# A fused attention and feed-forward kernel: turns of eight steps instead of four, V read per quad, two banks for set-aside scores, and the change of rows behind a GpSimd instruction

## The chip, the core and the metric

The kernel runs on one core of one Trainium2 chip. The metric is the device time of one execution in microseconds (us); lower is better. The engines are named as in the profile: PE (TensorE matmuls), PEld (its weight loads), DVE (VectorE), ACT (ScalarE), POOL (GpSimd) and SP (SyncE, which here only issues DMAs).

## What is computed

The layer norm of x feeds an attention of 32 heads of 16 dimensions over 2048 tokens, and a feed-forward part with squared ReLU that gates it:

```python
x = A_x                                    # [1, 2048, 512]
xn = _layernorm(x, axis=-1)
qkv = (xn @ wqkv) -> q, k, v               # H = 32 heads, Dh = 16
p = softmax(q @ k.T * Dh ** -0.5)
s = (p @ v) @ wo
r = relu(xn @ w1 + b1)                     # F = 1792
g = silu((r * r) @ w2 + b2)
out = x + s * g
```

Everything is fp32. Products of the linear parts and the scores are made with numbers split into a high and a low fp32r part (three products for one, hi-hi, hi-lo, lo-hi); the product of the exponentials with V is a plain fp32 matmul.

## The kernel before

**Setup** (to about 148 us) normalizes and transposes x, makes V, K and Q of all heads, keeps V in SBUF (tile `vt`, 16 key blocks of 560 columns: 17 per head, the 17th being one, which gives the softmax sums) and writes K and Q to memory.

**The loop.** Heads go by quads (four heads, 64 rows of K in split form for two of them, so that two heads' scores run side by side on the two halves of the PE array). A *step* is one quad, one block of 512 queries and one block of 128 keys: 8 x 4 x 16 = 512 steps. Each step has two *pairs* p = 0, 1, and each pair two halves `hp` (rows 0-63 and 64-127 of the array). `scores(i, p)` makes a direct pair into a two-bank PSUM tile S, of which there are two; `exps` then takes the exponential of the 1024 columns on ACT into a tile P in SBUF. `aside(i, p, hp)` makes one half of a pair into the single bank `lin`, and DVE copies it to P, where ACT later works in place. `values(i)` multiplies a step's four tiles with V; its 32-column tiles run four side by side and add up in the bank `acc` over the 16 key blocks.

The loop is written out by hand in *turns* of four steps (128 of them). A turn makes six direct pairs and two set-aside pairs; between them, `lin` issues products of the feed-forward part or of the output projection (*blocks*) on whichever half is given; the last two direct pairs are exponentiated while PE does the four steps' values. ACT's set-aside exponentials also run then. So PE alternates between a score part, on two 64-row halves, and a value part, on four 32-column tiles.

A pair of blocks fills two banks (`spare`). Half products of rows 0-63 of one block go to its bank while rows 64-127 of the other go to the other bank. `swap()` exchanges the rows. Before, `swap` falls on the end of a turn (a pair takes two turns), with the values between the two phases; a pair that must fit into one turn (`m == 1`, four times) gets two whole-array products (`issue_whole`) around the exchange. In other turns one product is cut into two pieces of 256 columns (`issue_part`). At the end of a pair `evict` runs on DVE: bias and ReLU, square, and the split of the hidden layer (low part on GpSimd), or the sum into `y`.

`fill` lists what a turn works on, `per` is its length for one block of 512 tokens, and `events` holds DMAs and small work by turn number (`at(time, ...)`, half numbers for after the products): loads of K (`load_ka`) and Q (`load_qa`), `split_piece` (weights cast on DVE, low part on GpSimd, next piece loaded), the row sums of the softmax (`finish`, `load_sums`, `rowsums`), the check of V's maximum (`maxvalue`), the gate (`gate_start` on ACT, `gate_end` on DVE). `see` makes ACT and DVE read one element of a tile, so that they have passed certain waits before the next instructions; which turns have it is chosen case by case.

`finish(i)` copies `acc` to `ou` once per block of queries, every fourth turn, on DVE or, in the turns with `turn_ends_first`, on ACT.

Of the kernel before, what the change touches and what calls it, by code (L numbers as in the profile page):

```python
# [36 lines left out]
NQ = H // 4  # L37
NC = S // 512
NK = S // 128
VW = 560  # L40
Z_MIN, BIG = 1e-18, 1e18
# [6 lines left out]
def mha_ffn_kernel(ctx: ExitStack, tc: tile.TileContext, x, wqkv, wo, bx, w1, b1, w2, b2, out):  # L48
# [8 lines left out]
    vt = keep.tile([128, NK, VW], FT, name="vt")  # L57
# [4 lines left out]
    qdram = [[dram.tile([128, 2, 512], FT, name=f"qd{g}_{c}") for c in range(NC)] for g in range(4)]  # L62
    xdram = [dram.tile([128, 2, 4, 512], FT, name=f"xd{c}") for c in range(3)]
# [7 lines left out]
    general_path(tc, dram, nvalid, ident, vt, kdram, qdram, gdram, x, wo, out)  # L71


def fast_path(tc, sb, ps, env):
    nc = tc.nc
    ident, vt, nvalid, stat = (env[n] for n in ("ident", "vt", "nvalid", "stat"))
    kdram, qdram, xdram, udram, zdram, gdram = (
        env[n] for n in ("kdram", "qdram", "xdram", "udram", "zdram", "gdram"))
# [4 lines left out]
    BUFS = dict(S=3, KA=3, QA=2, P=8, T=2, ou=2, wr=2, u=2, st=2, mv=2, rs=2, zc=2, rc=2)  # L83
# [68 lines left out]
    def split_w(which, ks=range(4), parts="hl"):  # L152
        if which not in wsp:
            tiles = [[t([128, 2, 512], FR, f"{w_tags[which]}{p}{i}") for i in range(2)] for p in "hl"]
            wsp[which] = [[a[k // 2][:, k % 2] for k in range(4)] for a in tiles]
# [90 lines left out]
    def end_value(c, i, v):  # L246
        pv = v[0]
        run(v[1])
        cast(act if i % 2 else dve,
             vt[:, 4 * c + i, :H * 17].rearrange("p (h e) -> p h e", e=17)[:, :, :DH],  # L250
             pv.rearrange("p (h e) -> p h e", e=DH))

    def keyquery(c, g, which, tag="S"):
# [4 lines left out]
        ev = t([128, 2, 512], FR, ("P2", "P3", "P4", "P0", "P5", "P1", "T", "T")[n] if c == 3 else f"P{n % 4}")  # L258
# [19 lines left out]

    steps = [(qd, qc, kb) for qd in range(NQ) for qc in range(NC) for kb in range(NK)]
# [12 lines left out]
    def place(i, p):  # L292
        ptile[i, p] = t([128, 2, 512], FT, f"P{2 * ((i - 1) % 4) + p}")
# [10 lines left out]
    def aside(i, p, hp):  # L304

        if hp == 0:
            place(i, p)
        score(i, p, hp, single)
        dve.tensor_copy(ptile[i, p][:, hp], single)  # L309
# [5 lines left out]
    class Block:  # L315
# [10 lines left out]
        def issue(self, half, bank):  # L326

            n, other = self.at[half], 1 - half
            if n == len(self.todo[half]):
# [4 lines left out]
            mm(bank, self.lhs(a, k)[r], self.rhs(b, k)[r], start=n == 0 and self.at[other] == 0,  # L334
               stop=n == len(self.todo[half]) - 1 and self.at[other] > 0)
            return True

        def issue_whole(self, bank):

            n = len(self.todo[0]) - 1  # L340
            k, a, b = self.todo[0].pop()
            assert (k, a, b) == self.todo[1].pop() and n in self.at and 0 in self.at
            mm(bank, self.lhs(a, k), self.rhs(b, k), start=False, stop=False)  # L343

        def issue_part(self, half, bank, part):

            n = self.at[half]
            if n >= len(self.todo[half]):
                return
            assert 0 < n < len(self.todo[half]) - 1  # L350
            k, a, b = self.todo[half][n]
            r, c = slice(64 * half, 64 * half + 64), slice(256 * part, 256 * part + 256)
            self.at[half] += part
            mm(bank[:, c], self.lhs(a, k)[r], self.rhs(b, k)[r, c], start=False, stop=False)  # L354
# [4 lines left out]
    pair, swapped = [None], [0]  # L359

    def lin(*halves):
        if pair[0]:
            for half in halves:
                j = half ^ swapped[0]
                pair[0][j].issue(half, lin_banks[j])

    def lin_part(half, part):
        if pair[0]:
            j = half ^ swapped[0]
            pair[0][j].issue_part(half, lin_banks[j], part)  # L370
# [30 lines left out]
    def split_piece(eng=None):  # L401
# [5 lines left out]
        wf[layer, m] = [t([128, 4, 256] if layer == 1 else [128, 2, 512], FR, f"wf{layer}{p}{q}") for p in "hl"]  # L407
# [40 lines left out]
    for c in ORDER:  # L448
        for m, (g, _) in enumerate(PAIRS):
            fill += [(lambda m=m: first(m), False), (None, True)]  # L450
            if m in (1, 2, 4, 6):
                for i in range(2):
                    make = lambda c=c, g=g if m > 1 else 0, i=i: second(c, g, i)
                    fill += [(make, True)] if m == 1 else [(make, False), (None, True)]
    per = len(fill) // NC
    fill = [(*a, n % per in (0, 2, 4, 5, 6, 8, 10, 12, 14, 16, 18, 20, 22, 24)) for n, a in enumerate(fill)]
# [6 lines left out]
    for i in range(4):  # L463
        part = vt[:, 4 * i:4 * i + 4]
        pool.memset(part[:, :, :H * 17].rearrange("p k (h e) -> p k h e", e=17)[:, :, :, DH:], 1.0)
        pool.memset(part[:, :, H * 17:], 0.0)
# [50 lines left out]
    for c in range(NC):  # L517
# [15 lines left out]
        for g in range(4):  # L533
# [15 lines left out]
            if g == 3 and c == 2:  # L549
                turn["KA"] = 1  # L550
                load_ka(0, 0)
                load_qa(0, 0)
            if g == 1 and c == 3:
# [11 lines left out]
    acc = [None]  # L565
# [484 lines left out]
```

## Time and profile before

| what | value |
|---|---|
| time, median of 3 runs | 1251.16 us (1250.55 to 1251.58) |
| profiled execution, its own time | 1251.08 us |
| its span | 1249.3 us |
| granted PE clock, mean | 0.997 |
| DMA moved | 137.28 MB, 84936 packets |

The span is what lies between the first and the last instruction that the profiler saw. In the groups by line, the columns are the line, the engine, the operation, what is written and read with its form, the count, then the busy time and the mean duration of one in nanoseconds, then the idle time of the engine before these instructions and what ended it. In the timeline the columns are start and duration in microseconds, engine, line, operation and tiles; `x3` joins three of them in a row. A plain fp32 matmul leaves two records, so that 16 value products are 32 of them.

### The profile page before, as it was taken

How to read it: one execution, taken by the hardware profiler on the slowest of the kernel's cores; microseconds unless marked ns; L12 is line 12 of the kernel's file. 1: busy time of each engine (PE TensorE's matmuls, PEld its weight loads, DVE VectorE, ACT ScalarE, POOL GpSimd, SP SyncE). 2: the span in 40 equal slices, each digit the busy share in tenths (PEclk: the TensorE clock that was granted, in tenths of full speed). 3: DMA queues.
4: the chain of work that ended last, by engine and by line, in shares of the span. 5: the costliest groups of instructions: out<-in, count | busy, mean ns of one | idle time of the engine just before them, and what ended most of it. 6: DMA issues, size and time to landing. Idle time of an engine off the chain costs nothing.

```text
span 1249.3 us, 24460 instructions
## 1 busy us (share of the span) xinstructions
PE 1238.0 (99%) x10029; PEld 718.9 (58%) x10029; DVE 692.9 (55%) x1274; ACT 1056.5 (85%) x1230; POOL 258.8 (21%) x151
## 2 busy tenths in 40 slices
PE   9999999999999999999999999999999999999997
PEld 8888755555555455555555555555555555555554
DVE  5543255555555655555565555555655545566655
ACT  4222599999999999999999999999999999999994
POOL 5000122122211221302023221220330212322112
PEclk9999999999999999999999999999999999999998
DMA  7555613231233232121423121332222122463445
GB/s 280 207 228 199 215 47 106 60 94 47 91 128 111 60 96 65 50 88 50 157 77 111 45 93 61 94 128 84 69 75 85 53 90 61 145 220 118 152 133 120
DMA packets 84936, 137.28 MB, mean 110 GB/s; under 512 B 26058, under 2 KB 40408, under 8 KB 83284
## 3 DMA queue, kind: packets, MB, share of 16 engines
q1 hardware_dynamic: 81668, 126.25, 31.5%
q0 software_dynamic: 2720, 8.65, 2.4%
q8 instruction: 79, 1.29, 0.4%
q10 hardware_dynamic: 432, 0.79, 0.2%
q14 instruction: 37, 0.30, 0.1%
HBM read 94.24 MB, written 41.41 MB: 109 GB/s over the span
## 4 chain that ended last, share of the span: by engine, by line
PE 98%; DVE 1%; ACT 0%; issue 0%; POOL 0%; DVEq 0%; POOLq 0%; ACTq 0%
PE acc L573 37%; PE spare L334 25%; PE S L286 16%; PE S L111 10%; PE lin L286 7%; PE spare L354 1%; PE lin L472 1%; PE S L208 0%; PE acc L111 0%; PE spare L343 0%; DVE P L309 0%; PE lin L111 0%; ACT P L290 0%; PE S L699 0%; PE acc L699 0%
## 5 line engine op out<-in xcount | busy, mean ns | idle before, releaser
L290 ACT ACTIVATE P<-S 128x1024 f32<-128x1024 f32 x768 | 733.1, 1020 | 39.5 <-PE S L286 38.4
L309 DVE COPY P<-lin 128x512 f32<-128x512 f32 x512 | 353.9, 691 | 312.9 <-PE lin L286 277.9
L573 PE MATMUL acc<-P,vt 128*32 128x512 f32 x4096 | 466.0, 595 | 0.0
L286 PE MATMUL S<-QA,KA 64*128 64x512 f32 x1536 | 335.5, 413 | 0.0
L290 ACT ACTIVATE P<-P 128x1024 f32<-128x1024 f32 x256 | 271.0, 1058 | 26.0 <-DVE P L309 19.3
L573 PEld LDWEIGHTS acc<-P,vt 128*32 128x32 f32 x4096 | 120.9, 109 | 264.8 <-issue 263.7
L286 PEld LDWEIGHTS S<-QA,KA 64*128 64x128 f32 x1536 | 153.8, 183 | 168.3 <-ACT P L290 128.1
L286 PE MATMUL lin<-QA,KA 64*128 64x512 f32 x512 | 204.0, 398 | 0.7 <-DVE P L309 0.4
L104 POOL TENSOR_TENSOR wf1l<-wr,wf1h 128x1024 fp32r<-128x1024 f32 x28 | 66.8, 2384 | 400.9 <-DVE wf1h L100 136.6
L104 POOL TENSOR_TENSOR hl<-T,hh 128x1024 fp32r<-128x1024 f32 x28 | 67.3, 2405 | 236.8 <-PE S L286 152.1
L104 POOL TENSOR_TENSOR wf2l<-wr,wf2h 128x1024 fp32r<-128x1024 f32 x28 | 66.6, 2380 | 201.2 <-PE acc L573 136.4
L334 PE MATMUL spare<-xl,wf1h 64*128 64x512 f32 x440 | 105.3, 391 | 0.0
L286 PEld LDWEIGHTS lin<-QA,KA 64*128 64x128 f32 x512 | 94.2, 184 | 17.6 <-DVE P L309 2.8
L334 PE MATMUL spare<-xh,wf1h 64*128 64x512 f32 x504 | 95.8, 390 | 0.0
L334 PE MATMUL spare<-xh,wf1l 64*128 64x512 f32 x504 | 95.6, 391 | 0.0
L334 PE MATMUL spare<-wf2l,hh 64*128 64x512 f32 x400 | 93.9, 391 | 0.0
L799 DVE TENSOR_TENSOR seen<-P,S 1x1 f32<-1x1 f32 x107 | 15.1, 141 | 137.6 <-ACT P L290 137.6
L334 PE MATMUL spare<-wf2h,hh 64*128 64x512 f32 x448 | 85.9, 390 | 0.0
L334 PE MATMUL spare<-wf2h,hl 64*128 64x512 f32 x416 | 80.9, 391 | 0.0
L334 PEld LDWEIGHTS spare<-xh,wf1h 64*128 64x128 f32 x504 | 59.9, 185 | 10.1
L98 ACT CAST P<-S 128x512 fp32r<-128x512 f32 x30 | 17.6, 587 | 56.7 <-PE S L111 54.9
L334 PEld LDWEIGHTS spare<-xh,wf1l 64*128 64x128 f32 x504 | 59.9, 185 | 7.5
(220 smaller groups left out, 1197.1 us busy)
## 6 DMA issues: line engine op xcount, KB each, us to landing
wr<-in_B_w_dram SPq DMA_DIRECT2D x56, 512.0 KB
KA<-kd SPq DMA_DIRECT2D x64, 256.0 KB
QA<-qd SPq DMA_DIRECT2D x128, 128.0 KB
kd<-P SPq DMA_DIRECT2D x15, 512.0 KB
qd<-P SPq DMA_DIRECT2D x15, 512.0 KB
u<-ud SPq DMA_DIRECT2D x15, 512.0 KB
P<-in_A_x_dram SPq DMA_DIRECT2D x8, 512.0 KB
xd<-KA SPq DMA_DIRECT2D x4, 1024.0 KB
```

Source lines behind the costliest of these rows:

```text
L98: act.copy(dst, src)
L104: leng.tensor_tensor(lo, src, hi.bitcast(FT), op=OP.subtract)
L111: mm(dst, lhs(a, k), rhs(b, k), start=n == 0, stop=n == len(todo) - 1)
L286: mm(dst, k[r, p, 128 * (kb % 8):128 * (kb % 8) + 128], q[r, p], start=True, stop=True)
L290: act.activation(ptile[i, p], src, AF.Exp, scale=SCALE)
L309: dve.tensor_copy(ptile[i, p][:, hp], single)
L334: mm(bank, self.lhs(a, k)[r], self.rhs(b, k)[r], start=n == 0 and self.at[other] == 0, stop=n == len(self.todo[half]) - 1 and self.at[othe ...
L354: mm(bank[:, c], self.lhs(a, k)[r], self.rhs(b, k)[r, c], start=False, stop=False)
L472: mm(idle[:, :128], ident, ident, start=True, stop=True)
L573: mm(acc[0][32 * j:32 * j + 32], vt[:, kb, o:o + 32], ptile[i, j // 2][:, j % 2], start=kb == 0, stop=kb == NK - 1)
L799: dve.tensor_tensor(seen[:, 8:9], last, other[:1, 0, :1], op=OP.max)
```

## The change

A turn has eight steps (64 turns). Its order is spelled in two strings: S a direct pair, L two half products, 0 and 1 a set-aside half beside a half product, B both set-aside halves of a pair, / the swap, E the end of a first pair of blocks. Eleven of the 16 pairs are direct and five set aside, the halves 0 in the bank `acc` and the halves 1 in `lin` (`sides`). The values of all eight steps follow and add up in `sides[0]`; ACT copies it to `ou` after each turn, and GpSimd adds the two of a block of queries. The swap comes in mid-turn, behind a one-element `memset` on GpSimd that waits for both blocks' products so far and for which the first products on the changed rows wait. There are 16 tiles of exponentials; to make room, V is written to memory in setup and loaded per quad, two buffers of 83 columns for each key block; the first layer's split weights have one buffer instead of two (with `split_piece` ahead of the eviction in turns that need it), and the normalized attention outputs have other tiles. `see` is the same in every turn. Events move to the new turn numbers.

```diff
+QW = 83
-    vt = keep.tile([128, NK, VW], FT, name="vt")
+    vdram = dram.tile([NK, 128, VW], FT, name="vd")
     def end_value(c, i, v):
         pv = v[0]
         run(v[1])
-        cast(act if i % 2 else dve,
-             vt[:, 4 * c + i, :H * 17].rearrange("p (h e) -> p h e", e=17)[:, :, :DH],
+        n = 4 * c + i
+        vb = vblocks[n % 6]
+        cast(act if i % 2 else dve, vb[:, :H * 17].rearrange("p (h e) -> p h e", e=17)[:, :, :DH],
              pv.rearrange("p (h e) -> p h e", e=DH))
+        sp.dma_start(vdram[n], vb)
...
+    def load_v(qd):
+        vq[qd] = t([128, NK, QW], FT, "V")
+        sp.dma_start(vq[qd], vdram[:, :, 68 * qd:68 * qd + QW].rearrange("k p e -> p k e"))
...
-        ptile[i, p] = t([128, 2, 512], FT, f"P{2 * ((i - 1) % 4) + p}")
+        ptile[i, p] = t([128, 2, 512], FT, f"P{2 * ((i - 1) % 8) + p}")
...
-        score(i, p, hp, single)
-        dve.tensor_copy(ptile[i, p][:, hp], single)
+        score(i, p, hp, sides[hp])
+        dve.tensor_copy(ptile[i, p][:, hp], sides[hp])
...
-            mm(bank, self.lhs(a, k)[r], self.rhs(b, k)[r], start=n == 0 and self.at[other] == 0,
-               stop=n == len(self.todo[half]) - 1 and self.at[other] > 0)
+            ins = mm(bank, self.lhs(a, k)[r], self.rhs(b, k)[r], start=n == 0 and self.at[other] == 0,
+                     stop=n == len(self.todo[half]) - 1 and self.at[other] > 0)
+            if n == 0 and self.at[other]:
+                tc.add_manual_dep(ins.ins, fence[0], SYNC, reason="the other rows of the bank")
+            self.last = ins.ins.name
...
     def swap():
         if pair[0]:
-            while any([pair[0][half ^ swapped[0]].issue(half, lin_banks[half ^ swapped[0]]) for half in range(2)]):
+            while lin(0, 1):
                 pass
-            swapped[0] ^= 1
-            if not swapped[0]:
-                pair[0][0].evict()
-                pair[0] = None
+            f = pool.memset(note, 0.0)
+            for block in pair[0]:
+                tc.add_manual_dep(f.ins, block.last, SYNC, reason="the products so far")
+            swapped[0], fence[0] = 1, f.ins.name
+
+    def end_pair():
+        if pair[0]:
+            while lin(0, 1):
+                pass
+            swapped[0], last, pair[0] = 0, pair[0], None
+            last[0].evict()
...
     def values(i):
         qd, qc, kb = steps[i]
-        if kb == 0:
-            acc[0] = t([128, 512], FT, "acc")
         for j in (1, 2, 3, 0) if i % 2 else (0, 1, 2, 3):
-            o = (4 * qd + j) * 17
-            mm(acc[0][32 * j:32 * j + 32], vt[:, kb, o:o + 32], ptile[i, j // 2][:, j % 2],
-               start=kb == 0, stop=kb == NK - 1)
+            mm(sides[0][32 * j:32 * j + 32], vq[qd][:, kb, 17 * j:17 * j + 32], ptile[i, j // 2][:, j % 2],
+               start=kb % 8 == 0, stop=kb % 8 == 7)
...
         ou = t([128, 512], FT, "ou")
-        cast(act if turn_ends_first[0] else dve, ou, acc[0])
+        act.copy(ou, sides[0])
+        if n % 2 == 0:
+            part[0] = ou
+            return
+        pool.tensor_tensor(ou, ou, part[0], op=OP.add)
...
-    def see(i, other, act_waits, dve_waits):
+    def see(i):
         last = ptile[i, 1][:1, 1, 511:]
-        if act_waits:
-            act.copy(seen[:, :1], last)
-        if dve_waits:
-            dve.tensor_tensor(seen[:, 8:9], last, other[:1, 0, :1], op=OP.max)
+        act.copy(seen[:, :1], last)
+        dve.tensor_tensor(seen[:, 8:9], last, sides[1][:1, :1], op=OP.max)
...
+    ORDINARY = "SLLSBLLLSLL0SL1LSLL/SBLLSLL0SL1LSLL0L1SLS"
+    TWO_PAIRS = "LSLLBLLLSS/L0LL1SLLESBSLLSLLLL/SBSLLL0LL1SS"
     for n in range(TURNS):
-        i = 4 * n
+        i = 8 * n
         happen(n)
...
+        if n:
+            see(i - 1)
+        pairs = [(k, p) for k in range(i + 1, i + 9) for p in range(2)]
+        direct, asides = pairs[:9] + pairs[14:], pairs[9:14]
+        later, aside_at = [], [0, 0]
+        for row in TWO_PAIRS if makes else ORDINARY:
+            if row == "S":
+                k, p = direct.pop(0)
+                sc = scores(k, p)
+                if k == i + 8:
+                    later.append((k, p, sc))
+                else:
+                    exps(k, p, sc)
+            elif row == "L":
+                lin(0, 1)
+            elif row in "01B":
+                for hp in (0, 1) if row == "B" else (int(row),):
+                    aside(*asides[aside_at[hp]], hp)
+                    aside_at[hp] += 1
+                if row != "B":
+                    lin(1 - int(row))
+            elif row == "/":
+                swap()
+                if n == TURNS - 1:
+                    make_on(2, 3)
+            else:
+                end_pair()
+                pair[0] = makes.pop(0)()
+        for j, (k, p) in enumerate(asides):
+            exps(k, p, ptile[k, p])
+            if j == 0:
+                for fn, a in middle.pop(n, ()):
+                    fn(*a)
+        for a in later:
+            exps(*a)
...
+        pieces_now = pieces_of[n] if n < len(pieces_of) else 0
+        ahead = pieces_now > 0 and n % per in (0, 1, 3, 6, 7, 10, 11)
+        while lin(0, 1):
+            pass
+        if ahead:
+            split_piece()
+        end_pair()
...
         happen(n + 0.5)
-        if split_now:
+        for _ in range(pieces_now - ahead):
             split_piece()
-        for j in range(4):
+        for j in range(8):
             values(i + j)
-        if early:
-            see(i + 4, last[1], False, alone[1])
-            alone[1] = False
-        finish(i + 3)
+        finish(n)
...
     for s in half:
-        act.copy(ou[:, s], acc[0][:, s])
+        dve.tensor_tensor(ou[:, s], sides[0][:, s], part[0][:, s], op=OP.add)
```

More of the change, by code (lines that the diff above doesn't have):

```diff
@@ L776, in fast_path @@
     lin_banks = [spare[:, 0], spare[:, 1]]
-    single = t([128, 512], FT, "lin")
+    sides = [t([128, 512], FT, "acc"), t([128, 512], FT, "lin")]
     xs[0] = xT[3]
@@ L811, in fast_path @@
-        if make:
-            pair[0] = make()
-        pair0 = scores(i + 1, 0)
-        if n:
-            see(i, last[1], *now)
-        exps(i + 1, 0, pair0)
-        aside(i + 3, 0, 0)
-        lin(1)
-        lin(0, 1)
-        exps(i + 1, 1, scores(i + 1, 1))
-        for _ in range(2):
-            lin(0, 1)
-        lin(0)
-        if make and end:
-            lin(1)
-            lin(0)
-            aside(i + 3, 0, 1)
-        else:
-            lin_part(1, 0)
-            aside(i + 3, 0, 1)
-            lin(0)
```

191 lines of the change are left out of this document (69 added, 122 removed).

## The prediction

> **What bounds the kernel now.** I read the head of the page first, then the chain of waits, then the groups by form:
>
> ```profile
> span 1249.3 us, 24460 instructions
> PE 1238.0 (99%) x10029; PEld 718.9 (58%) x10029; DVE 692.9 (55%) x1274; ACT 1056.5 (85%) x1230; POOL 258.8 (21%) x151
> PE 98%; DVE 1%; ACT 0%; issue 0%; POOL 0%; DVEq 0%; POOLq 0%; ACTq 0%
> ...
> L290 ACT ACTIVATE P<-S 128x1024 f32<-128x1024 f32 x768 | 733.1, 1020 | 39.5 <-PE S L286 38.4
> ```
>
> PE looks like the only bound: 99% busy, 98% of the chain. But a busy PE may hide waits, since ends of matmuls are modelled, and ACT is 85% busy although its exponentials start only near 148 us. So I took one four-step turn from the timeline, PE's rows and then ACT's:
>
> ```profile
> 602.27 3.64 PE L573 MATMUL acc<-P,vt 128*32 128x512 f32 x32
> 605.84 0.50 PE L286 MATMUL S<-QA,KA 64*128 64x512 f32 x2
> 606.18 0.62 PE L334 MATMUL spare<-wf2h,hh 64*128 64x512 f32 x3
> ...
> 606.88 0.62 PE L334 MATMUL spare<-wf2h,hh 64*128 64x512 f32 x4
> ...
> 608.50 0.40 PE L286 MATMUL S<-QA,KA 64*128 64x512 f32 x2
> 609.43 0.40 PE L286 MATMUL S<-QA,KA 64*128 64x512 f32 x2
> 610.35 0.41 PE L286 MATMUL S<-QA,KA 64*128 64x512 f32 x2
> 610.69 3.64 PE L573 MATMUL acc<-P,vt 128*32 128x512 f32 x32
> ```
>
> ```profile
> 602.88 1.06 ACT L290 ACTIVATE P<-P 128x1024 f32<-128x1024 f32 x1 [0.17 <-DVE P L309]
> 603.85 1.92 ACT L290 ACTIVATE P<-S 128x1024 f32<-128x1024 f32 x2
> 605.80 0.19 ACT L797 COPY seen<-P 1x1 f32<-1x1 f32 x1
> 606.38 3.80 ACT L290 ACTIVATE P<-S 128x1024 f32<-128x1024 f32 x4 [0.40 <-PE S L286]
> 610.07 1.06 ACT L290 ACTIVATE P<-P 128x1024 f32<-128x1024 f32 x1
> ```
>
> Call s the start of a turn's first score pair S1, here 605.84. The first exponential starts at s+0.54; four take 610.07 - 606.38 = 3.69, so 0.92 each, and one lasts 1.02 (the group's mean). There are two score buffers, so a pair waits for the exponential two before it. Exponentials 2, 3 and 4 end at s+2.48, 3.40 and 4.32; pairs S4, S5, S6 start at s+2.66, 3.59 and 4.51: 0.18 or 0.19 behind each. So the second half of the score part goes at ACT's pace. The values follow 0.34 behind S6 and last 3.57 until the next S1. Sum: 0.54 + 3 x 0.92 + 1.02 + 0.19 + 0.34 + 3.57 = 8.42, which is 610.69 - 602.27. That chain, and not the shares of busy time, is what I carry over. PE's own pace shows where it does not wait: a slot (two half-array matmuls side by side) takes (606.88 - 606.18)/3 = 0.233, and the first of a turn 0.34.
>
> **An ordinary turn after the change.** Eight steps have 11 direct pairs, 10 set-aside halves and 48 half products: 80 half matmuls in 40 slots, then 64 value records. The two 256-column pieces per block pair go, and one of every two changes between scores and values.
>
> ACT first. Each turn now ends with ACT's copy of the values' bank, and the one-element copy `see` stands behind it on the same queue. The trace has such a copy in 15 turns:
>
> ```profile
> 214.62 0.13 PEld L573 LDWEIGHTS acc<-P,vt 128*32 128x32 f32 x4 [0.30 <-issue]
> ...
> 215.05 0.13 PEld L573 LDWEIGHTS acc<-P,vt 128*32 128x32 f32 x4 [0.30 <-issue]
> ...
> 216.88 0.50 PE L286 MATMUL S<-QA,KA 64*128 64x512 f32 x2
> ...
> 217.02 0.59 ACT L98 COPY ou<-acc 128x512 f32<-128x512 f32 x1 [0.21 <-PE acc L573]
> ...
> 217.50 1.03 ACT L290 ACTIVATE P<-S 128x1024 f32<-128x1024 f32 x1
> ```
>
> The copy starts at s+0.14 and gives ACT back 0.48 later. `see` then costs 0 (all overlapped) to 0.19 (its row); I take 0.17, near the row. So exponential 1 starts at s+0.79. Nine direct exponentials run before the last pair, S11, may start: 0.79 + 8 x 0.92 + 1.02 + 0.19 = s+9.36; values at s+9.70.
>
> PE on its own: 0.34 + 38 x 0.233 + 0.34 = s+9.53. But the order string puts S6 only three slots behind S5, and S6 needs exponential 4: 0.79 + 3 x 0.92 + 1.02 + 0.19 = s+4.76. Twenty slots later, at s+9.42, comes S11, and the values at s+9.76. So PE and ACT are matched to 0.06; I take the later. The values are 3.57 and, for 32 more records at 0.43 per four (215.05 - 214.62), 8 x 0.43 = 3.43: 7.00. **The turn is 16.76, against 2 x 8.42 = 16.84.** One change of parts fewer is nearly eaten by ACT's later start (0.79 for 0.54).
>
> **What lies beside it.** ACT's remaining work fits into the values: five exponentials of set-aside tiles at 0.97 (603.85 - 602.88) end near s+13.9, the eighth step's values begin at s+9.76+6.0 = 15.8, and the two last direct ones end near s+15.8, 1.0 before the values do. A tanh of 1 us still fits. DVE, set-aside copies:
>
> ```profile
> L309 DVE COPY P<-lin 128x512 f32<-128x512 f32 x512 | 353.9, 691 | 312.9 <-PE lin L286 277.9 <-PE spare L334 32.3 <-ACT P L290 2.6
> ...
> L417 DVE TENSOR_SCALAR T<-spare,b1t 128x512 f32<-128x512 f32 x56 | 38.9, 731 | 0.0
> L418 DVE TENSOR_TENSOR T<-T 128x1024 f32<-128x1024 f32 x28 | 34.3, 1225 | 1.0
> L433 DVE TENSOR_TENSOR y<-spare,y 128x1024 f32<-128x1024 f32 x24 | 28.8, 1202 | 0.0
> ...
> L100 DVE CAST hh<-T 128x1024 fp32r<-128x1024 f32 x28 | 19.4, 694 | 1.7 <-DVE T L418 0.5
> ...
> L607 DVE RECIPROCAL rc<-zc 32x64 f32<-32x64 f32 x31 | 16.4, 530 | 0.0
> ```
>
> Ten copies of 0.69 are 6.9 in a score part of 9.8, and with two banks none is needed sooner than seven slots after the one before it in that bank, or three behind a single copy: enough. After the last product DVE evicts the hidden layer and casts up to two weight pieces: 2 x 0.73, 1.23 and three casts of 0.69, from s+9.8 to about 14.6; row sums add a reciprocal of 0.53 and two small reductions, about 1 (estimate). The maximum of V falls into turns that evict only `y` (1.20). So DVE is free 1 us before the next turn and over 2 before that turn's first set-aside copy. GpSimd's splits and its new sum of two `ou` end by about 2 us into the next turn: the second split waits for a cast until s+14, the third ends near s+18.8.
>
> **The GpSimd instruction.** The swap now comes mid-turn: a one-element memset waits for both blocks, and the first products on the changed rows wait for it; behind these stands all of PE's queue, and behind that ACT. The last product before it starts at 0.34 + 17 x 0.233 = s+4.30 and ends 0.39 later, 4.69. S6 and two set-aside halves come between, so the product would load its weights at about 4.76 + 2 x 0.233 - 0.12 = 5.11. The handshake has 0.42. No row shows PE waking GpSimd, so bounds from the nearest rows:
>
> ```profile
> 0.26 0.09 POOL L1037 MEMSET const-float32-0.0<- 128x1 f32 x1 [0.26 <-issue]
> ...
> 1.03 0.29 POOL masks.py:199 TENSOR_SCALAR_AFFINE_SELECT ident<-ident 128x128 f32<-128x128 f32 x1
> ...
> 1.37 6.52 PEld L472 LDWEIGHTS lin<-ident 128*128 128x128 f32 x32 [1.37 <-POOL ident masks.py:199]
> ...
> 8.07 0.55 DVE L190 TENSOR_SCALAR T<-P,mv,rs 128x512 f32<-128x512 f32 x1
> ...
> 8.68 0.18 POOL L479 COPY okm<-T 128x1 f32<-128x1 f32 x1 [6.12 <-DVE T L190]
> ...
> 182.12 0.70 DVE L100 CAST hh<-T 128x1024 fp32r<-128x1024 f32 x1
> ...
> 182.96 2.39 POOL L104 TENSOR_TENSOR hl<-T,hh 128x1024 fp32r<-128x1024 f32 x1 [8.84 <-PE S L286]
> ```
>
> DVE wakes GpSimd in 0.06 (8.62 to 8.68) to 0.14 (182.82 to 182.96); a tiny instruction takes 0.09 to 0.18; PE starts 0.05 behind GpSimd (1.32 to 1.37). Together 0.20 to 0.37: hidden, at a cost of 0, with as little as 0.05 to spare. It cannot bring a gain; above, it costs what it exceeds 0.42 by, in each turn.
>
> **Four turns with two block pairs.** Here S2 stands in the ninth slot, at 0.34 + 7 x 0.233 = s+1.97, so exponential 2 starts 0.54 later, at 2.5 and not 1.7 (0.8 lost), and the second pair's first product waits some 0.2 for the eviction of the first (1.20, L433). I take 17.8 each.
>
> **The rest.** V now goes to memory in setup and is read per quad, 4.5 turns (75 us) ahead; QA has 1.5 turns. These add SP issues, which wait in no one's way; were V late, PE would stand still for that load alone. But turn 0 now reaches key block 8 at its end, near 157 us, and that half of K is issued at:
>
> ```profile
> 147.94 0.50 PE L286 MATMUL S<-QA,KA 64*128 64x512 f32 x2
> ...
> 149.85 2.56 SPq L269 DMA_DIRECT2D KA<-kd  x4
> ...
> L573 PEld LDWEIGHTS acc<-P,vt x4096: 105/110/111, 153.4 to 1231.6; 128*32 128x32 f32 x196
> ```
>
> That leaves 4.6 us to land: 0 to 1 us once, I take 0. The last partial sum goes through DVE instead of ACT: 0.1.
>
> **Sum.** The loop of before runs from 147.94 to about 1232.6 (last record 1231.6 plus a drain of 1): 1084.7. After: 60 x 16.76 + 4 x 17.8 = 1076.8, and 0.6 because the first turn's score part was 5.45 long (147.94 to 153.4) instead of 4.85. That is 7.3 less. The profiled execution took 1251.08, 0.08 under the median of 1251.16: 1243.8, so **1244**. Its own range: `see` at nothing brings S6 to 4.59 and a turn to 16.59, 60 x 0.17 = 10 less: 1234. Irregular turns, of which before has some 2 us, reach 1248.
>
> **Rivals.**
> 1. *The GpSimd instruction holds PE.* For it: only 0.05 spare by the upper bounds, and no row of PE waking GpSimd. Against: every bound still fits. From a handshake of 0.53 the gain is gone (68 swaps x 0.11 = 7.5); at 0.6 to 0.8 it costs 68 x 0.18 to 0.38, so 1256 to 1270. 22%, of which 8% stays within the noise. This is the case on the other side.
> 2. *DVE is late with the set-aside copies.* Slack is 2 us by the rows; if first-layer turns (28) overran it by 0.6, 17 us: 1261. 10%, of which 2% ends at no change.
> 3. *GpSimd's own work runs late and the memset queues behind it.* Rows of the end:
>
> ```profile
> L104 POOL TENSOR_TENSOR wf2l<-T,wf2h 128x512 fp32r<-128x512 f32 x7 | 9.0, 1283 | 20.3 <-DVE wf2h L100 20.3
> ...
> L933 POOL TENSOR_TENSOR P<-P,KA 128x512 f32<-128x512 f32 x1 | 1.7, 1661 | 0.0
> ```
>
> A subtraction of one shape takes 1.28; a sum of that shape beside DVE's sums of two SBUF operands took 1.66. The sum of `ou` starts at 0.14 + 0.59 = s+0.73 and ends at 2.0, stretched at 2.4; in the four turns with two pairs the last product before the first swap ends at 0.34 + 6 x 0.233 + 0.39 = s+2.1, so the memset can be late. With the splits ahead stretched too, 1 to 3 us in each of four turns: 1248 to 1256. 7%, of which 4% is no change. The Trainium skill (GPSIMD Engine Reference, Specifications) says that GpSimd shares its SBUF interfaces with VectorE and contends with its instructions of two SBUF inputs; the 1661 ns agree.
> 4. *The order binds less than I think,* PE overtaking at S6: 1228 to 1234. For it, only the 0.27 that PE would save there. 3%.
>
> **How the numbers follow.** Forecast 58%. Faster by over 0.2% (below 1248.7; about what a measurement here tells from no change): 58 and rival 4's 3, 0.61; within it 8 + 2 + 4, 0.14; slower 14 + 8 + 3, 0.25. The range 1234 to 1262 leaves out the upper part of rival 1 and rival 4.
>
> **What would show it.** Values of 7.0, starting every 16.7 to 16.8 us; ACT's first exponential 0.8 behind S1; S11 0.19 behind the ninth exponential's end. Wrong, if PE's weight loads wait for GpSimd's memset for more than 0.1, or idle behind DVE's copies at the first set-aside halves.

## The result, and the profile after

| | before | after |
|---|---|---|
| median | 1251.37 us (4 runs) | 1239.70 us (4 runs, 1238.94 to 1240.35) |
| ratio of the times | | 0.9907, 95% interval 0.9889 to 0.9924 |
| profiled span | 1249.3 us | 1237.8 us |

The change makes the kernel 0.9% faster. The forecast was 1244.0, the range 1234 to 1262. So the time is 4.3 us under the forecast and within the range. The head of the page after, its chain and the largest group:

```profile
span 1237.8 us, 24227 instructions
PE 1219.9 (99%) x9925; PEld 716.1 (58%) x9925; DVE 778.5 (63%) x1230; ACT 1039.6 (84%) x1235; POOL 321.6 (26%) x254
PE 93%; DVE 2%; ACT 2%; DMA 1%; issue 1%; POOL 0%; SPq 0%; DVEq 0%; POOLq 0%; ACTq 0%
...
L300 ACT ACTIVATE P<-S 128x1024 f32<-128x1024 f32 x704 | 656.3, 1014 | 6.8 <-PE S L296 6.7
```

PE is again 99% busy, now of a span 11.5 us shorter. DVE's busy time has grown by 86 us although it has fewer instructions; the set-aside copies account for 353.9 us before and 440 after (221.2 for bank `acc`, 219.2 for `lin`), as much as that growth. What else came and went on DVE cancels out, though it holds 28 us more for the squares of the hidden layer (last section). The chain is less PE's alone: 93% instead of 98%.

One ordinary turn from the timeline (start, duration, engine, line, operation, tiles; in brackets the idle time before and its releaser). Its first score pair S1 starts at 615.57, the next turn's at 632.13:

```profile
615.57 0.50 PE L296 MATMUL S<-QA,KA 64*128 64x512 f32 x2
615.71 0.59 ACT L581 COPY ou<-acc 128x512 f32<-128x512 f32 x1 [0.24 <-PE acc L571]
616.20 0.18 ACT L791 COPY seen<-P 1x1 f32<-1x1 f32 x1
616.29 8.29 ACT L300 ACTIVATE P<-S 128x1024 f32<-128x1024 f32 x9
616.37 0.39 PE L296 MATMUL S<-QA,KA 64*128 64x512 f32 x2
...
619.38 0.40 PE L296 MATMUL S<-QA,KA 64*128 64x512 f32 x2
...
619.61 0.63 PE L344 MATMUL spare<-xh,wf1l 64*128 64x512 f32 x4
...
620.06 0.19 PEld L296 LDWEIGHTS S<-QA,KA 64*128 64x128 f32 x2 [0.26 <-ACT P L300]
620.07 0.49 PE L296 MATMUL S<-QA,KA 64*128 64x512 f32 x2
...
620.37 0.09 POOL L370 MEMSET note<- 1x1 f32 x1 [2.69 <-PE spare L344]
620.40 0.39 PE L296 MATMUL acc<-QA,KA 64*128 64x512 f32 x1
...
620.51 0.31 PEld L344 LDWEIGHTS spare<-xh,wf1h 64*128 64x128 f32 x4 [0.15 <-POOL note L370]
620.63 0.63 PE L344 MATMUL spare<-xh,wf1h 64*128 64x512 f32 x4
...
624.79 0.40 PE L296 MATMUL S<-QA,KA 64*128 64x512 f32 x2
625.13 0.16 PEld L571 LDWEIGHTS acc<-P,V 128*32 128x32 f32 x8 [0.32 <-DVE P L319]
...
632.13 0.50 PE L296 MATMUL S<-QA,KA 64*128 64x512 f32 x2
```

The turn lasts 632.13 - 615.57 = 16.56. ACT's first exponential starts at s+0.72, S6 at s+4.50, the memset at s+4.80, S11 at s+9.22 and the values at s+9.56; they last 7.00 until the next S1. From the second pair to the fifth, PE goes through 13 slots in 619.38 - 616.37 = 3.01: 0.2315 each. At S6 the weight load waits for ACT until 620.06 and the matmul follows at once; the slot after S6 comes 0.33 later (620.40) instead of 0.23.

The medians over the 52 turns 5 to 56, worked out from the same rows of the timeline: 16.62 for a turn, 9.61 of it from S1 to the values and 7.00 from the values to S1. Two kinds of turn alternate: in turns like the one shown the first exponential starts at s+0.72 and the values at s+9.57, in those between at s+0.77 and s+9.62 (medians); what makes that first 0.05 was not looked for. The four two-pair turns take 17.57 to 17.59. Five turns are irregular: 16.92 (turn 3), 19.11 (54), 17.78 (57), 17.64 (61) and 17.04 (63).

### The profile page after: what moved, and what is told of

Its sections match the earlier page's. It is cut to its first block, busy times and chain, and to the rows that moved or that the text cites. A ratio compares the mean times of both kernels' runs of the same rounds, so it can differ in the third digit from the quotient of the medians.

```text
span 1237.8 us, 24227 instructions
## 1 busy us (share of the span) xinstructions
PE 1219.9 (99%) x9925; PEld 716.1 (58%) x9925; DVE 778.5 (63%) x1230; ACT 1039.6 (84%) x1235; POOL 321.6 (26%) x254
## 4 chain that ended last, share of the span: by engine, by line
PE 93%; DVE 2%; ACT 2%; DMA 1%; issue 1%; POOL 0%; SPq 0%; DVEq 0%; POOLq 0%; ACTq 0%
PE acc L571 35%; PE spare L344 27%; PE S L296 14%; PE S L112 10%; PE acc L296 4%; PE lin L296 2%; ACT P L300 2%; PE S L210 1%; PE acc L112 0%; DMA gl<-gd 0%; POOL xl L105 0%; DMA P<-in_A_x_dram 0%; DVE P L319 0%; PE lin L112 0%; DVE wf2l L101 0%
## 5 line engine op out<-in xcount | busy, mean ns | idle before, releaser
L300 ACT ACTIVATE P<-S 128x1024 f32<-128x1024 f32 x704 | 656.3, 1014 | 6.8 <-PE S L296 6.7
L571 PE MATMUL acc<-P,V 128*32 128x512 f32 x4096 | 452.7, 594 | 0.0
L319 DVE COPY P<-acc 128x512 f32<-128x512 f32 x320 | 221.2, 691 | 313.5 <-PE lin L296 203.5
L300 ACT ACTIVATE P<-P 128x1024 f32<-128x1024 f32 x320 | 310.9, 1060 | 0.0
L571 PEld LDWEIGHTS acc<-P,V 128*32 128x32 f32 x4096 | 126.5, 110 | 289.3 <-issue 268.1
L319 DVE COPY P<-lin 128x512 f32<-128x512 f32 x320 | 219.2, 685 | 1.6 <-PE lin L296 0.6
L296 PE MATMUL lin<-QA,KA 64*128 64x512 f32 x320 | 125.9, 394 | 1.8 <-DVE seen L792 1.8
L296 PE MATMUL acc<-QA,KA 64*128 64x512 f32 x320 | 125.5, 392 | 0.3 <-DVE T L105 0.3
L585 POOL TENSOR_TENSOR ou<-ou,ou 128x512 f32<-128x512 f32 x31 | 40.4, 1303 | 142.7 <-ACT seen L791 142.6
L296 PEld LDWEIGHTS acc<-QA,KA 64*128 64x128 f32 x320 | 59.0, 184 | 11.7 <-DVE P L319 0.8
```

Of the source, the lines that this page charges most:

```text
L296: mm(dst, k[r, p, 128 * (kb % 8):128 * (kb % 8) + 128], q[r, p], start=True, stop=True)
L300: act.activation(ptile[i, p], src, AF.Exp, scale=SCALE)
L319: dve.tensor_copy(ptile[i, p][:, hp], sides[hp])
L571: mm(sides[0][32 * j:32 * j + 32], vq[qd][:, kb, 17 * j:17 * j + 32], ptile[i, j // 2][:, j % 2], start=kb % 8 == 0, stop=kb % 8 == 7)
L585: pool.tensor_tensor(ou, ou, part[0], op=OP.add)
```

## The experiments

All times are medians; each ratio is to the kernel before, on the same chip, with its 95% interval. "The turn" is the median distance from one turn's first values to the next one's.

**A longer memset.** Does the GpSimd instruction stand on the path?

```diff
-    note = t([1, 1], FT, "note")
+    note = t([128, 192], FT, "note")
...
+            f = pool.memset(note, 0.0)
```

> The GpSimd part of the swap is made longer: two memsets of 128x192 in a row instead of one of 1x1, so some 0.3 to 0.5 us more between the products of the two phases. Theory: the handshake has 0.05 to 0.15 us to spare and nothing behind it absorbs more, so each of 68 swaps lengthens by 0.2 to 0.4 us: 1254 to 1267 us. Rival (PE waits for ACT anyway at S7 to S11, which absorbs it): within 3 us of 1239.7.

It took 1267.53 us, ratio 1.0123 (1.0106 to 1.0139). The two memsets last 0.26 each, the weights behind them load 0.49 later (s+5.43), and the turn grows by 0.42, to 17.04; the time is half a microsecond above the expected range. The waits of this kernel:

```profile
PEld spare L344 <- POOL note L373: 42.0, 66, 2.5
```

66 weight loads wait for it, 42.0 us in all; with the instruction of the change it is 24 loads and 6.4 us, of which one alone is 2.0 (turn 54). So rival 1's mechanism is real: what the handshake takes beyond its room is paid in nearly every turn. The room left is 0.49 - 0.42 = 0.07, close to the least of the forecast (0.05).

**ACT earlier, and S6 later.** If S6 waits for the fourth exponential, either should shorten the turn.

```diff
-        act.copy(seen[:, :1], last)
```

> ACT's one-element copy at the turn's start is left out. Matched-chain theory (ACT's first exponential sets S6, and S6 sets the values): exponential 1 starts 0.09 us earlier, S6 and the values too, so an ordinary turn goes from 16.62 to 16.53 us and the kernel from 1239.7 to about 1234. Rival (PE's own slots set the turn): exponential 1 earlier, the turn still 16.62, 1240 us.

1239.86 us, 0.9906 (0.9890 to 0.9923), turn 16.59. The first exponential comes 0.09 earlier, and the turn gains 0.03 only: a miss. But the fourth exponential ends only 0.03 earlier (s+4.46 instead of 4.50), since the first four end 0.917 apart here and 0.904 apart in the change (medians). So S6 and the values move with the fourth exponential's end, and not with the first one's start.

```diff
-    ORDINARY = "SLLSBLLLSLL0SL1LSLL/SBLLSLL0SL1LSLL0L1SLS"
+    ORDINARY = "SLLSBLLLSLL0SL1LSLL/BSLLLSLL0SL1LSL0L1SLS"
```

> The second half of the ordinary order is BSLLLSLL0SL1LSL0L1SLS instead of SBLLSLL0SL1LSLL0L1SLS: pairs S6 to S9 stand one slot later, the same 40 slots. Theory: S6, three slots behind S5, waits for ACT and pushes the twenty slots behind it; one slot later it waits about 0.2 us less, and the values start at S1 + 9.5 instead of 9.61: turn 16.5, about 1233 us. Rival (nine exponentials before S11 alone set the values' start): no change, 1240 us.

1239.87 us, 0.9905 (0.9889 to 0.9922), turn 16.60: a miss again. Its rows show why:

```profile
620.34 0.52 PE L296 MATMUL S<-QA,KA 64*128 64x512 f32 x2
620.40 0.09 POOL L370 MEMSET note<- 1x1 f32 x1 [2.67 <-PE spare L344]
...
620.54 0.58 PEld L344 LDWEIGHTS spare<-xh,wf1h 64*128 64x128 f32 x6
620.58 0.98 PE L344 MATMUL spare<-xh,wf1h 64*128 64x512 f32 x6
```

S6 no longer waits for ACT's exponential, but the first product behind the swap now starts 0.04 behind its own weight load instead of 0.12: the load, at s+4.94 in both kernels because the memset comes no earlier, has become the late one. One late weight load was exchanged for two: the slot behind that first product takes 0.31 instead of 0.23, and S11, now 0.11 behind the ninth exponential, is followed by the values after 0.38 instead of 0.33 (medians).

**What a change between scores and values costs.** S11 is put between the fourth and fifth step's values, which adds two changes of form.

```diff
+            if j == 4:
+                k, p = direct.pop(0)
+                exps(k, p, scores(k, p))
             values(i + j)
```

> The last direct pair S11 is issued between the values of the fourth and the fifth step, so that every turn has two more changes between scores and values, as the kernel before had in eight steps. Theory: S11's slot (0.23) leaves the score part and comes back as a change into and out of scores (0.14 + 0.34): +0.25 us per turn, 16.87, 1256 us. Rival (the change of form is free, and S11's wait for exponential 9 was the bound): the values start 0.2 us earlier and the turn is 16.6 or less, 1238 us or less.

1259.92 us, 1.0065 (1.0048 to 1.0082), turn 16.95. The score part is one slot shorter (9.38 for 9.61, which is 0.23), the values with the slot in them 0.57 longer (7.05 for 6.48 from the first to the last of a turn's value matmuls). So two changes of form cost 0.57 - 0.23 = 0.34 beside the slot's own work. The turn grows by 0.33, where 0.25 was expected.

**One bank for all set-aside scores.**

```diff
-        score(i, p, hp, sides[hp])
-        dve.tensor_copy(ptile[i, p][:, hp], sides[hp])
+        score(i, p, hp, sides[1])
+        dve.tensor_copy(ptile[i, p][:, hp], sides[1])
```

> All set-aside halves go through the one bank `lin`, as in the kernel before; the values keep `acc`. Theory: a half in the same bank must wait for the copy of the one before, 0.39 + 0.04 + 0.69 + 0.05 = 1.2 us behind it; the two halves of a B stand in one slot, the others 2 to 3 slots (0.5 to 0.7 us) apart, so a turn loses 2 to 4 us: 1370 to 1500 us. Rival (DVE is idle enough, the second bank buys little): under 0.5 us per turn, 1240 to 1272 us.

1515.42 us, 1.2114 (1.2094 to 1.2135), turn 20.92: 4.3 a turn, a little above the expectation. PE waits for the bank:

```profile
PEld lin L296 <- DVE P L319: 323.8, 389, 1.7
```

Without the second bank the turns of eight would lose far more than they bring.

**The partial sum copied by DVE instead of ACT.**

```diff
-        act.copy(ou, sides[0])
+        dve.tensor_copy(ou, sides[0])
```

> The copy of the values' bank to `ou` goes from ACT to DVE, as in most turns of the kernel before. ACT's first exponential then starts near S1 + 0.55 instead of 0.75. Theory (the GpSimd handshake lets the first product behind the swap load at S1 + 4.94 whatever ACT does): ordinary turns 16.55 to 16.62, and late set-aside copies where DVE is full: 1238 to 1243 us. Rival (ACT's late start costs each turn): 16.4, 1226 to 1231 us.

1240.60 us, 0.9918 (0.9902 to 0.9935). ACT starts at s+0.54, 0.20 earlier, and the turn stays at 16.56 or 16.63. Here 62 weight loads wait for the memset, 15.8 us in all, and the slot behind the first swapped product takes 0.31 instead of 0.23. So the handshake took about half of what ACT gave; the rest went to two slots that are some 0.03 longer, one behind the first set-aside pair (whose bank DVE now empties of the values first) and one behind S6 (medians).

**V streamed, and nothing else of the change.** The kernel before, with V in memory and read per quad:

```diff
-    vt = keep.tile([128, NK, VW], FT, name="vt")
+    vdram = dram.tile([NK, 128, VW], FT, name="vd")
...
+        sp.dma_start(vdram[n], vb)
...
+    def load_v(qd):
+        vq[qd] = t([128, NK, QW], FT, "V")
+        sp.dma_start(vq[qd], vdram[:, :, 68 * qd:68 * qd + QW].rearrange("k p e -> p k e"))
```

> The kernel before with one part of the change alone: V written to memory in setup and loaded per quad (two buffers), with one maximum per quad; turns of four steps as before. Theory: free, 1250 to 1253 us. Rivals: its DMAs disturb others, over 1254 us; or part of the gain comes from it, under 1249 us.

1252.07 us, 1.0007 (0.9998 to 1.0017): no cost that shows.

**The late turns.** In turn 54, DVE has an output weight piece of `split_wo` behind the hidden layer, and GpSimd two `xl` subtractions ahead of the sum of `ou` and the memset; in turn 57, DVE comes late to its set-aside copies because `maxvalue(7)` (1.47) stands among its other work; in turn 61 DVE waits for a gate's load. The three are moved:

```diff
-... if n >= LAST or n % per in (4, 5, 9, 12, 13)]) + 0.5, maxvalue, qd)
+... if n > LAST or n % per in (4, 5, 9, 12, 13)]) + 0.5, maxvalue, qd)
...
-        at(LAST - 2.5, split_wo, i)
+        at(LAST - 2.5 + i, split_wo, i)
...
-        at(LAST + 4 + n - 0.5 * (n > 0), load_gate, c, i, "gl")
+        at(LAST + 4 + n - (0.5 if n else 1), load_gate, c, i, "gl")
```

> Three events are moved: the second half of the split of wo one turn later, the last maximum of V one turn later, the first load of a gate half a turn earlier. Theory: the turns of 19.1, 17.8 and 17.6 us are late because GpSimd or DVE is late at the next set-aside copy or swap; they go to 16.6, 3 to 5 us less: 1235 to 1237 us. Rival (something else holds these turns): 1240 us.

1238.58 us, 0.9898 (0.9881 to 0.9914): less than expected. The three turns are back at 16.6, but turn 55 takes 20.74. In it DVE waits for the normalized outputs' load, whose buffer the second piece of wo, now a turn later, still held:

```profile
1068.48 0.69 DVE L674 TENSOR_TENSOR T<-u 128x512 f32<-128x512 f32 x1 [3.52 <-DMA u<-ud]
```

So those loads were moved too:

```diff
-        at(LAST - 2 + n // 2, load_on, c, g)
-        at(LAST - 1.5 + n // 2, make_on, c, g)
+        at(LAST - 2 + (n + 1) // 2, load_on, c, g)
+        at(LAST - 1.5 + (n + 1) // 2, make_on, c, g)
```

> As in e7, and the loads of the attention's outputs for the last projections one turn later for every second one, so that no load waits in SP's queue for the buffer that the second half of wo still holds. Theory: the turn of 20.7 us that e7 brought goes to 16.6 and its three mended turns stay so: 4 to 5 us under the changed kernel, 1234.5 to 1236 us. Rival (the lateness moves to another turn again): 1238 us or more.

1235.54 us, 0.9873 (0.9857 to 0.9890). Turns 54 to 62 are now 16.49 to 16.63; of the end, only turn 63 is late (18.11, against 17.04 in the change; 1.2 of it is a wait for DVE behind `make_on`). This version beats both kernels; the rest of the runs start from it.

**Both waits off at once.** `see` without ACT's copy, and S6 later, in this version:

```diff
-        act.copy(seen[:, :1], last)
...
-    ORDINARY = "SLLSBLLLSLL0SL1LSLL/SBLLSLL0SL1LSLL0L1SLS"
+    ORDINARY = "SLLSBLLLSLL0SL1LSLL/BSLLLSLL0SL1LSL0L1SLS"
```

> e9 with ACT's one-element copy left out and S6 to S9 one slot later together, so that neither ACT's start nor S6's place holds PE. Theory (the handshake over GpSimd lets the first product behind the swap load at S1 + 4.93 in every order): the ordinary turn stays at 16.55 to 16.62 and the time within 2 us of e9. Rival (each of the two edits only uncovered the other's wait): 16.5 us, 6 us under e9.

1239.84 us, 0.9910 (0.9893 to 0.9926), turn 16.66. The theory's 2 us were missed (it is 4.3 slower), and the rival's gain is not there either. With S6 later the sixth exponential starts at s+5.36 instead of 5.30, and the ninth at s+8.15 instead of 8.01, although the first began 0.09 earlier: S6 feeds ACT, and S11 now waits for the ninth.

**The handshake shorter.** After these runs my theory was that three limits lie within 0.1 of each other: S6 behind the fourth exponential, the memset, and S11 behind the ninth. So the memset went to DVE, which is idle there:

```diff
-    def swap():
+    def swap(eng=None):
...
-            f = pool.memset(note, 0.0)
+            f = (eng or pool).memset(note, 0.0)
...
-                swap()
+                swap(dve if len(fill[n]) == 1 else pool)
```

> This is e9 with one difference: in the ordinary turns the small memset that stands between the products of the low rows and the loading of the swapped weights is done by DVE instead of GpSimd (the two-pair turns keep it on GpSimd). In e9 the last product ahead of it ends 4.665 us after the turn's first score step, the memset starts 0.13 later, lasts 0.09, and the weights load at 4.94. DVE is idle around 4.5 to 5.2, and elsewhere in the trace it starts about 0.04 behind the end it waits for, with about 0.06 for a tiny operation: the weights would load at about 4.82. Theory (three limits lie within 0.1 us of each other: step 6 behind the fourth exponential, the handshake, step 11 behind the ninth exponential): turn 16.58 to 16.61, 1234 to 1236 us. Rival (the handshake alone sets the turn): turn 16.49, about 1229 us.

> e11 with ACT's copy of the seen statistics left out as well (the copy is of no use to the output), so that the first exponential comes 0.09 us earlier and the fourth with it. Theory (three limits): all three are loosened by 0.09 to 0.12 us at once, turn about 16.50, 1229 to 1232 us. Rival (the handshake is no limit, or something else than these three sets the turn): turn 16.59 to 16.62, no better than e9's 1235.5 us.

The first took 1235.53 us, 0.9870 (0.9854 to 0.9887), turn 16.62; the second, without ACT's copy `seen`, 1235.45 us, 0.9873 (0.9857 to 0.9890), turn 16.59. Rows of the first, in the turn shown above (S1 at 615.67):

```profile
620.40 0.06 DVE L370 MEMSET note<- 1x1 f32 x1 [0.25 <-PE spare L344]
620.50 0.39 PE L296 MATMUL acc<-QA,KA 64*128 64x512 f32 x1
...
620.51 0.41 PEld L344 LDWEIGHTS spare<-xh,wf1h 64*128 64x128 f32 x4
620.73 0.64 PE L344 MATMUL spare<-xh,wf1h 64*128 64x512 f32 x4
```

The weight load waits for nobody now, and comes a slot ahead of its product. Yet the product starts at s+5.06, as it did behind GpSimd (620.63 - 615.57 = 5.06). The medians over the turns say the same: s+5.11 behind GpSimd and s+5.11 behind DVE. The handshake on GpSimd therefore costs nothing in an ordinary turn. With ACT's copy left out too, the turn gains 0.03 and not 0.10, and the rival's "16.59 to 16.62" holds. This was a smaller loosening than planned: as before, the fourth exponential ends only 0.03 earlier, and S6 and the values follow it by that much.

So two of the three limits are none in an ordinary turn: the memset, and S11, which starts 0.21 to 0.24 behind the ninth exponential. S6 behind the fourth exponential is one. PE's own pace would be 0.34 + 38 x 0.2315 + 0.34 = 9.48 for the score part. In the change S6 starts on that pace in every second turn and 0.05 behind it in the others, and the slot after it is 0.10 longer in all: 9.58 and 9.63, measured 9.57 and 9.62. The second kernel here has 9.54 and 9.59.

What ACT alone would allow stands in turn 56 of the change, which has six slots fewer, so that PE stands still and waits for ACT at S6 and at S11:

```profile
1085.07 0.50 PE L296 MATMUL S<-QA,KA 64*128 64x512 f32 x2
1085.78 8.28 ACT L300 ACTIVATE P<-S 128x1024 f32<-128x1024 f32 x9
1089.56 0.50 PE L296 MATMUL S<-QA,KA 64*128 64x512 f32 x2 [0.40 <-ACT P L300]
1094.12 0.50 PE L296 MATMUL S<-QA,KA 64*128 64x512 f32 x2 [0.23 <-ACT P L300]
1094.55 0.64 PE L571 MATMUL acc<-P,V 128*32 128x512 f32 x4
```

S11 starts at 1094.12, 0.06 behind the ninth exponential's end (1085.78 + 8.28; 0.05 before rounding, and 0.05 at S6): that is what a release takes here. The values start at s+9.49, 0.43 behind S11, whose weights are late too. So PE's pace alone allows 9.48 and ACT's chain alone 9.49, and together they take about 0.1 more.

No order tried here takes away that last 0.10 without a like loss elsewhere. One that might was not run: S6 later together with the memset on DVE. In the run with S6 later the late load behind the swap cost 0.08 a turn, so some 5 us over 60 turns (an estimate).

## Why the prediction came out

**The direction was right, and the kind of reasoning too:** a turn worked out from the starts of its pieces, not from busy shares, and the GpSimd instruction hidden. From s to the values it was 0.15 too long. That the total came within 4.3 us is luck in part, since two errors of opposite sign met: 9.4 us too much for the regular turns and those with two pairs, and 4.7 too little for five irregular turns that the forecast did not have. The account against the forecast's loop of 1077.4, from the first loop pair at 147.94 to the last value's end at 1220.43, which is 1072.5:

| part | forecast | measured | difference, us |
|---|---|---|---|
| first score part | 10.36 | 10.07 | -0.3 |
| 54 regular turns | 16.76 each | 16.60 each (mean) | -8.5 |
| four two-pair turns | 17.8 each | 17.58 each | -0.9 |
| five irregular turns | 16.76 each | 88.49 together | +4.7 |
| last values | 7.00 | 7.07 | +0.1 |
| sum | 1077.4 | 1072.5 | -4.9 |

After the loop, 17.4 us remain where before had 16.7: +0.7 instead of the forecast's 0.1, so the difference of the spans is 12.2 - 0.7 = 11.5. That tail was not taken apart.

**The step that was mis-sized is S6's wait.** The forecast had S6 at s+4.76, behind the fourth exponential, and let 20 slots follow. The median is s+4.55 (4.51 and 4.55 in alternate turns). In the turns with 4.55 the 0.21 has four pieces: the first exponential starts at s+0.77 instead of 0.79 (0.02; `see` hands ACT on 0.09 after its start, not 0.17, but the copy starts later); three more at 0.909 instead of 0.92 (0.03); the fourth lasts 1.00 instead of 1.02 (0.02); and S6 follows 0.05 behind its end instead of 0.19. This last one, 0.14, is the largest.

The 0.19 goes back to a wrong reading of the turn of before, that the second half of its score part goes at ACT's pace. Its rows between S4 (608.50) and S5 (609.43):

```profile
608.50 0.40 PE L286 MATMUL S<-QA,KA 64*128 64x512 f32 x2
608.74 0.39 PE L334 MATMUL spare<-wf2l,hh 64*128 64x512 f32 x1
...
609.43 0.40 PE L286 MATMUL S<-QA,KA 64*128 64x512 f32 x2
609.67 0.84 PE L334 MATMUL spare<-wf2h,hl 64*128 64x512 f32 x5
```

From S4 to S5 and from S5 to S6 are four slots each, in 0.93 and 0.92: 0.23 a slot, PE's own pace, and the slots behind S4 and S5 come after 0.24, so no weights were late. All 20 slots at that pace are 0.34 + 18 x 0.2315 + 0.34 = 4.85, which is the whole score part. So no pair waited in that turn, and the 0.19 was only where PE happened to be; the sum of 8.42 came out because the 0.19 had been read from the same turn. In the turn after, six of the other eight pairs that have a pair's exponential two before them also start 0.19 to 0.23 behind an exponential (medians), and none of them waits. Against the 0.21 stands the slot behind S6, 0.10 longer than the forecast's, since weights that wait for ACT are not loaded ahead.

**PE's own pace, which the forecast had at 9.53 and set aside for the later 9.76, is the nearer bound:** 9.48, and 9.61 in the median with S6's wait. The pitch of the exponentials from the second on is 0.904 here and was 0.92 before; what shortens it stays open. It did not decide anything at S11, which starts 0.23 behind the ninth exponential's end, more than a release needs.

**The values** were right: 7.00. The gain of a turn, 16.84 to 16.60, lies about half in the values (2 x 3.57 = 7.14 to 7.00) and half in the score part (2 x 4.855 = 9.71 to 9.61). The two changes of form that a turn saves are worth 0.34 when S11 is put among the values. At PE's pace alone the turn would be 9.48 + 7.00 = 16.48, 0.36 less than before; ACT's later start, through S6, takes 0.14 of it back, and not nearly all, as the forecast had it.

**The handshake**, forecast at 0.20 to 0.37: the last product before the swap ends at s+4.67, the memset starts 0.13 later, lasts 0.09, and the weights load 0.05 behind its end (medians): 0.27. GpSimd took 0.13 to wake behind PE, near the upper bound that I had from DVE; DVE in its place took 0.06. The cost of 0 holds (the memset on DVE shows it), and so does the small room (the longer memset shows it). The forecast's sign of being wrong, weight loads that wait over 0.1 for the memset, did appear (0.15 in the turn shown), but it was no good sign: a weight load that waits costs PE nothing while it still comes ahead of its matmul.

**The rivals.** The first did not happen but its price was of the right kind: 0.49 more of handshake gave 0.42 a turn. The second and the third happened, in another place than I had put them: not in the 28 first-layer turns and not in the two-pair turns, but in turn 54. There both queues carry the work of the output projection as well:

```profile
1043.32 2.41 POOL L105 TENSOR_TENSOR wf2l<-wr,wf2h 128x1024 fp32r<-128x1024 f32 x1 [5.72 <-DVE wf2h L101]
1047.62 2.76 POOL L105 TENSOR_TENSOR hl<-T,hh 128x1024 fp32r<-128x1024 f32 x1 [1.89 <-DVE hh L101]
1050.35 5.19 POOL L105 TENSOR_TENSOR xl<-u,xh 128x1024 fp32r<-128x1024 f32 x2
1055.48 1.28 POOL L585 TENSOR_TENSOR ou<-ou,ou 128x512 f32<-128x512 f32 x1
1056.69 0.09 POOL L370 MEMSET note<- 1x1 f32 x1
```

```profile
1051.04 0.18 PEld L296 LDWEIGHTS lin<-QA,KA 64*128 64x128 f32 x1 [0.72 <-DVE seen L792]
...
1056.84 0.30 PEld L344 LDWEIGHTS spare<-wf2h,hh 64*128 64x128 f32 x4 [2.01 <-POOL note L370]
```

GpSimd works without a gap from 1047.62, so the memset is 2 us late, and PE's queue waits 2.01 behind its weight load; earlier in the turn it had waited 0.72 for DVE. That is rival 3's mechanism and some of rival 2's, 2.5 us in one turn. The forecast's row for a stretched sum, 1661 ns, was not what it took it for: GpSimd ran there from 1240.27 to 1241.93, mostly beside two DVE instructions with one operand in PSUM, and DVE's sum of two SBUF operands began only at 1241.32. What made that row long stays open. The forecast counted no such turn, and the moved events took 4.2 us out of the whole. The fourth rival, with 3%, came about in the ordinary turns: its 1228 to 1234 are 10 to 16 us less over 60 turns, a turn of 16.50 to 16.60, and the mean is 16.60, because S6 hardly waits. The five irregular turns kept the whole out of its range. The low end of the forecast's own range, a turn of 16.59, had this size too, but for another reason (`see` at nothing).

## What to carry to other kernels

- Read the time that a release needs from the shortest distance in the trace, not from a typical one: pairs that started 0.19 behind an exponential were not waiting for it at all, as counting the slots between them would have shown, and PE's own pace was the nearer bound.
- When two limits come out within a few hundredths of each other, loosening one shows little; lengthen the suspect instead (the longer memset), or take it away altogether (the memset on another engine), and read where the instruction behind it starts. A turn in which one of the two has less to do (turn 56) shows the other alone.
- When turns get twice as long, list what each queue has to do in the busiest turns, and not only in the ordinary ones: 54 ordinary turns brought 13 us here (0.24 each), and five irregular ones cost 5.5 of it (88.49 - 5 x 16.60).

## What the hardware showed that was not expected

**DVE and GpSimd take turns.** In the change, the weights' split stands ahead of the eviction, so that GpSimd subtracts while DVE squares the hidden layer. All 28 squares of one shape, whose mean before was 1225 ns:

```profile
L420 DVE TENSOR_TENSOR T<-T 128x1024 f32<-128x1024 f32 x28 | 62.7, 2240 | 1.0
...
L105 POOL TENSOR_TENSOR hl<-T,hh 128x1024 fp32r<-128x1024 f32 x28 | 80.1, 2860 | 52.9 <-DVE seen L792 30.2
```

```profile
1043.15 1.40 DVE L419 TENSOR_SCALAR T<-spare,b1t 128x512 f32<-128x512 f32 x2
1044.59 2.22 DVE L420 TENSOR_TENSOR T<-T 128x1024 f32<-128x1024 f32 x1
1046.84 0.69 DVE L101 CAST hh<-T 128x1024 fp32r<-128x1024 f32 x1
1047.45 3.48 DVE L101 CAST xh<-u 128x1024 fp32r<-128x1024 f32 x2
1050.85 0.14 DVE L792 TENSOR_TENSOR seen<-P,lin 1x1 f32<-1x1 f32 x1
```

GpSimd's subtraction began at 1043.32 and ended at 1045.73. The square, begun at 1044.59, ended 1.08 behind that, a little less than its work takes alone (1.23): it did nothing until GpSimd was through. In all 28 cases that distance is 1.08 or 1.09. Of the two casts of `u`, the first took its 0.69 and the second 2.88, until 0.55 behind the end of GpSimd's next subtraction (1050.38). GpSimd waits in the same way: that subtraction, whose like took 2.40 in the kernel before, took 2.76 and ended 2.24 behind the first cast (1048.14). Eleven others of the 28 took 3.41 to 3.97; each ran beside DVE's row sums and a cast or a sum, and ended 2.24 to 2.27 behind the latter. The biases' sums read PSUM (1.40 for two, 1.39 before) and were not held up. The Trainium skill (SBUF — State Buffer, SBUF: two separate sides) says that the port pair which the two engines share is an exclusive lock, held for a whole instruction by whichever starts first, and not a split of bandwidth; the 1.08 and the 0.55 agree. The forecast had reckoned with a stretch in GpSimd's sums and costed the square at 1.23. The missing 1.0 us in each of 28 turns cost nothing there, since DVE is idle behind it, as in this one:

```profile
577.60 2.21 DVE L420 TENSOR_TENSOR T<-T 128x1024 f32<-128x1024 f32 x1
579.84 0.69 DVE L101 CAST hh<-T 128x1024 fp32r<-128x1024 f32 x1
580.45 0.14 DVE L792 TENSOR_TENSOR seen<-P,lin 1x1 f32<-1x1 f32 x1
583.81 0.69 DVE L319 COPY P<-acc 128x512 f32<-128x512 f32 x1 [3.23 <-PE lin L296]
```

But DVE stood behind that lock when it was late in turn 54.

**A weight load that comes late costs 0.10,** even when the data come in time for the matmul. In the turn shown S6 starts 0.23 behind the slot ahead of it, as it should, but the next slot starts 0.33 behind S6. The load had come 0.01 ahead of its matmul. In the turn of before, S5's load waited for ACT too, but came 0.11 ahead (609.32 for 609.43), and the next slot followed after 0.24.
